# Fused chunk attention and swish MLP: a start-up wait moved behind a second load, and PV of one unit joined to the scores of the next from unit 14 on

## The chip, the cores and the metric

One core of a Trainium2 chip. The metric is the device time of one execution in microseconds (us). Lower is better. Each version was run several times on a chip beside runs of the kernel before; medians of all its runs are quoted with their number. A run is called fast or slow by its granted clock and by its distance from the fastest run of the same kernel.

## The reference, cut to what matters

```python
# q, k, v: (8, 8, 576, 64) float32; chunks of 64 positions attend within themselves
q_c = q.reshape(B, H, nc, chunk, D)          # the same for k_c, v_c; nc = 9
scores = scale * np.matmul(q_c, k_c.transpose(0, 1, 2, 4, 3))
attn = softmax(scores)                        # written out in the reference
out = np.matmul(attn, v_c).reshape(B, H, S, D)
x = out.transpose(0, 2, 1, 3).reshape(4608, 512)
h = x @ w_in                                  # (512, 2048)
g = h * (1.0 / (1.0 + np.exp(-beta * h)))
result = g @ w_out                            # (2048, 512), float32
```

## The kernel before

The 4608 tokens are worked in 18 units of 256, and the MLP in 9 blocks of two units. Everything is one static order. While TensorE works through the first layer of block j (`hps`) and the second layer of block j-1 (`ops`), pieces of the attention of later units are put in between: scores (`sc`), then PV (attention weights times v, into `x` or `y`). From unit 8 on both use the array as 64 x 64; the MLP uses it as 128 x 128. ScalarE makes the exponentials and the sigmoid, VectorE normalises and multiplies, and in the blocks shown below transposes go by DMA. GpSimd issues most loads. The results of the large matmuls go to a pool of four buffers (`ps_p`), called banks below.

The part that puts pieces in place, for blocks 3 to 8. The number at the head of each item is a place within the block, from 0 to 1:

```python
        def att_items(u, a0, w):
            return [(a0, 2, ("sc", u)), (a0 + 0.40 * w, 3, ("pv", u)),
                    (a0 + 0.41 * w, 3, ("norm", u, 0)), (a0 + 0.55 * w, 3, ("norm", u, 1)),
                    (a0 + 0.10 * w, 3, ("T", u + 1))]

        for j in range(3, NB):
            items = [(0.02 + 0.98 * m / KFF, 0, ("m", m)) for m in range(KFF)]
            # ... the second layer of block j-1, in eight parts ...
            if j + 1 < NB:
                for i in range(2):
                    items += att_items(2 * j + 2 + i, 0.03 + 0.43 * i, 0.43)
            items.sort(key=lambda it: it[:2])
            # ... each item is emitted in this order ...
```

The start. `emit_idle` and `emit_tiny` are matmuls on zeros that keep TensorE busy ahead of the first scores; the one that reads `late` waits for GpSimd's memset. In the kernel before, idle matmuls of 512 columns start 0.43 us apart up to about 7.7 us and 0.216 apart from 8.78 us on. Where this text says that the clock doubled, it means this change of spacing at the start: the granted clock of the profile reads 1.00 through the same twelve microseconds. That the idle matmuls bring the doubling on is what they are put there for.

```python
        # ... SyncE loads the first halves of q, k; GpSimd the second halves; SyncE beta ...
        nc.gpsimd.memset(late, 0.0)
        for i in range(4):
            load_v(i)
        # ... GpSimd: weights and further loads ...
        emit_tiny(78)
        warm = idle_bank()
        emit_idle(3, 512, warm)
        nc.tensor.matmul(out=warm[:, 0:16], lhsT=idle[:, 0:128], rhs=late)
        emit_idle(10, 512, warm)
        emit_T_half(0)          # ScalarE casts, VectorE transposes the first halves
        emit_sc_half(0, 0)      # 32 small matmuls
        emit_ex_half(0, 0)
        warm = idle_bank()
        emit_idle(6, 512, warm)
        emit_T_half(1)          # VectorE transposes the second halves
        nc.vector.transpose(out=bt, in_=braw)
        emit_sc_half(0, 1)
```

The softmax here doesn't subtract the row's maximum and nothing guards it: scores larger than these inputs give would overflow.

## Time and profile before

| | kernel before |
|---|---|
| median of 3 runs (lowest to highest) | 289.49 us (289.14 to 290.41) |
| span of the profiled run | 287.5 us |
| TensorE busy | 281.2 us, 98% |
| VectorE, ScalarE busy | 141.4 and 146.7 us, 49% and 51% |
| first large first-layer matmul starts | 15.62 us |
| last group of second-layer matmuls starts | 280.80 us |

How to read it: from 17 us to the end TensorE hardly ever stands still, so its stream is the bound. The start of the first large matmul says what the start-up cost. The start of the last group says where the stream ended, for the tail behind it is the same in every version (6.6 to 6.7 us to the end of the span in the seven that are read at this point: before, after, e2, e3, e4, e8 and e12). These are the two rows, in order of time (start, duration to the modelled end, engine, line, operation, tiles, shape, count, and in brackets the idle time before it with what ended it):

```profile
15.62 1.03 PE L322 MATMUL hps<-xt,win 128*128 128x256 f16 x8 [0.67 <-ACT xt L297]
280.80 3.70 PE L580 MATMUL ops<-wout,gt 128*128 128x256 f16 x48
```

Their distance is 265.18 us.

### The profile page before, as it was taken

How to read it: one execution, taken by the hardware profiler on the slowest of the kernel's cores; microseconds unless marked ns; L12 is line 12 of the kernel's file. 1: busy time of each engine (PE TensorE's matmuls, PEld its weight loads, DVE VectorE, ACT ScalarE, POOL GpSimd, SP SyncE). 2: the span in 40 equal slices, each digit the busy share in tenths (PEclk: the TensorE clock that was granted, in tenths of full speed). 3: DMA queues.
4: the chain of work that ended last, by engine and by line, in shares of the span. 5: the costliest groups of instructions: out<-in, count | busy, mean ns of one | idle time of the engine just before them, and what ended most of it. 6: DMA issues, size and time to landing. Idle time of an engine off the chain costs nothing.

```text
span 287.5 us, 6650 instructions
## 1 busy us (share of the span) xinstructions
PE 281.2 (98%) x2779; PEld 136.2 (47%) x2779; DVE 141.4 (49%) x253; ACT 146.7 (51%) x224; POOL 95.7 (33%) x125
## 2 busy tenths in 40 slices
PE   8889999999999999999999999999999999999995
PEld 4464456545544444444444444444444444444444
DVE  2678444776567554534454445444453536333300
ACT  4377218774557545454545454555445544444411
POOL 8743579397172992060907060000000000000000
PEclk9999999999999999999999999999999999999999
DMA  8999999999999999999999999614252212010012
GB/s 197 174 197 206 169 178 209 211 163 173 153 94 182 155 176 179 153 130 159 132 167 134 145 155 142 134 49 110 75 113 73 73 39 73 36 39 36 36 73 75
DMA packets 139997, 37.14 MB, mean 129 GB/s; under 512 B 126912, under 2 KB 135488, under 8 KB 139968
## 3 DMA queue, kind: packets, MB, share of 16 engines
q0 software_dynamic: 99136, 17.83, 79.7%
q1 hardware_dynamic: 40688, 18.83, 30.5%
q8 instruction: 22, 0.36, 0.5%
q14 instruction: 7, 0.06, 0.1%
q10 hardware_dynamic: 144, 0.07, 0.1%
HBM read 36.71 MB, written 9.44 MB: 161 GB/s over the span
## 4 chain that ended last, share of the span: by engine, by line
PE 94%; DMA 3%; ACT 1%; issue 1%; DVE 0%; POOL 0%; DVEq 0%; POOLq 0%
PE hps L322 44%; PE ops L354 42%; DMA h<-in_k_dram 3%; PE x L264 2%; PE sc L236 1%; PE sc L223 1%; PE ops L580 1%; ACT xt L297 1%; PE xp L296 1%; PE sc L196 0%; ACT et L206 0%; POOL h L394 0%; PE warm L374 0%; PE xp L304 0%; DVE xt L297 0%
## 5 line engine op out<-in xcount | busy, mean ns | idle before, releaser
L336 DVE SCALAR_TENSOR_TENSOR gt<-sg,hps 128x512 f16<-128x512 f32 (+1 forms) x153 | 99.1, 654 | 108.5 <-ACT sg L332 108.3
L332 ACT ACTIVATE sg<-hps,beta 128x512 f32<-128x512 f32 (+1 forms) x153 | 100.4, 663 | 74.0 <-PE hps L322 73.9
L322 PE MATMUL hps<-xt,win 128*128 128x512 f16 (+1 forms) x612 | 136.7, 367 | 0.8 <-ACT xt L297 0.7
L354 PE MATMUL ops<-wout,gt 128*128 128x512 f16 x560 | 131.3, 379 | 0.0
L322 PEld LDWEIGHTS <-win 128*128 128x128 f16 x612 | 58.0, 98 | 61.9 <-issue 1.0
L354 PEld LDWEIGHTS <-gt 128*128 128x128 f16 x560 | 53.7, 98 | 63.1
L364 ACT ACTIVATE osb<-ops 128x512 f32<-128x512 f32 x35 | 20.9, 598 | 42.2 <-PE ops L354 42.2
L112 POOL DMA_DIRECT2D vbig<-in_v_dram x40 | 34.0, 872 | 10.3 <-DMA wout<-in_moe_w_out_dram 3.7
L98 POOL DMA_DIRECT2D qu<-in_q_dram x22 | 18.7, 865 | 39.5 <-DMA qT<-qu 37.2
L280 DVE TENSOR_TENSOR x<-x,rd 128x512 f16<-128x512 f32 x34 | 23.5, 692 | 1.3
L98 POOL DMA_DIRECT2D ku<-in_k_dram x22 | 18.9, 880 | 0.1
L278 DVE RECIPROCAL rd<-x 128x8 f32<-128x8 f32 x34 | 6.8, 201 | 11.1 <-PE x L264 11.1
L245 ACT ACTIVATE et<-sc 128x1024 f16<-128x1024 f32 (+1 forms) x8 | 6.4, 811 | 8.2 <-PE sc L236 8.2
L229 ACT ACTIVATE et<-sc 128x1024 f16<-128x1024 f32 x10 | 10.1, 1015 | 0.0
L264 PEld LDWEIGHTS <-et 64*64 64x64 f16 x576 | 6.0, 107 | 7.3 <-issue 3.4
L374 PE MATMUL warm<-idle 128*128 128x512 f16 x24 | 8.6, 515 | 0.0
L264 PE MATMUL x<-vbig,et 64*64 64x65 f16 x544 | 7.8, 195 | 0.2 <-ACT et L206 0.2
L104 POOL DMA_DIRECT2D ku<-in_k_dram x9 | 6.8, 755 | 2.5 <-DMA win<-in_moe_w_in_dram 1.3
L104 POOL DMA_DIRECT2D qu<-in_q_dram x9 | 6.8, 767 | 1.9 <-DMA win<-in_moe_w_in_dram 1.1
L592 DVE TENSOR_SCALAR osb<-ops 128x256 f32<-128x256 f32 (+1 forms) x2 | 0.7, 358 | 12.1 <-PE ops L580 12.1
L130 POOL DMA_DIRECT2D win<-in_moe_w_in_dram x8 | 6.0, 751 | 1.2 <-DMA h<-in_k_dram 0.8
L177 DVE STREAM_TRANSPOSE t<-h 128x512 f32<-128x512 f32 x4 | 4.2, 1084 | 4.2 <-ACT h L176 3.7
(46 smaller groups left out, 69.3 us busy)
## 6 DMA issues: line engine op xcount, KB each, us to landing
out_dram<-osb SPq DMA_DIRECT2D x35, 256.0 KB, 3.4
vbig<-in_v_dram POOLq DMA_DIRECT2D x32, 128.0 KB, 7.6
qu<-in_q_dram POOLq DMA_DIRECT2D x20, 128.0 KB, 5.3
ku<-in_k_dram POOLq DMA_DIRECT2D x20, 128.0 KB, 6.6
win<-in_moe_w_in_dram POOLq DMA_DIRECT2D x8, 256.0 KB, 9.7
wout<-in_moe_w_out_dram POOLq DMA_DIRECT2D x4, 512.0 KB, 12.4
qu<-in_q_dram POOLq DMA_DIRECT2D x3, 256.0 KB, 7.3
ku<-in_k_dram POOLq DMA_DIRECT2D x3, 256.0 KB, 8.9
```

The costliest lines, as they stand in the source:

```text
L98: nc.gpsimd.dma_start(out=tv[off:off + n, sp], in_=src[b, :, s:s + n, :].rearrange("h p d -> p h d"),)
L104: nc.gpsimd.dma_start(out=t[off // 2:(off + n) // 2], in_=src[b, :, s:s + n, :].rearrange("h (p r) d -> p h r d", r=2),)
L112: nc.gpsimd.dma_start(out=vbig[off:off + n, i, :, 0:D], in_=v[b, :, s:s + n, :].rearrange("h p d -> p h d"),)
L229: nc.scalar.activation(out=et, in_=sc, func=ACTF.Exp, scale=scale)
L264: nc.tensor.matmul(out=(x[0][64 * c:64 * c + 64, r, g, 0:D + 1] if len(x) == 1 else x[r][64 * c:64 * c + 64, g, 0:D + 1]), lhsT=(et[64 * r ...
L280: nc.vector.tensor_tensor(out=o, in0=z[..., 0:D], in1=rd[:, r].to_broadcast(list(o.shape)), op=ALU.mult)
L322: nc.tensor.matmul(out=hps[:, 0:n], lhsT=w_in16[m // 2][:, kk, (m % 2) * 128:(m % 2) * 128 + 128], rhs=xr[:, c0 // CH:(c0 + n) // CH, 2 * ...
L332: nc.scalar.activation(out=sg[:, 0:n], in_=hps[:, 0:n], func=ACTF.Tanh, scale=beta2[:, m:m + 1])
L336: nc.vector.scalar_tensor_tensor(out=gt_t[j][:, m, c0:c0 + n], in0=sg[:, 0:n], scalar=1.0, in1=hps[:, 0:n], op0=ALU.add, op1=ALU.mult,)
L354: nc.tensor.matmul(out=ops, lhsT=gt_t[j][:, kk, t * 128:(t + 1) * 128], rhs=w_out16[kk // 4][:, kk % 4, :], start=(kk == 0), stop=(kk == K ...
L364: nc.scalar.activation(out=osb, in_=ops, func=ACTF.Copy, scale=0.5)
L374: nc.tensor.matmul(out=d[:, 0:w], lhsT=idle[:, 0:128], rhs=idle[:, 0:w])
```

## The change

Its intent: (1) to hold part of the start-up idle work back, so that TensorE's idle matmuls reach up to the first scores, and (2) to let PV of a unit and scores of the next share one passage between the 128 x 128 and the 64 x 64 use of the array, from unit 14 on. The diff, its core:

```diff
+    MU = 14
...
     def emit_pv(u, where=("x", "s")):
         et = et_t.pop(u)
-        for s in range(2):
+        for s in (1, 0) if u >= MU else (0, 1):
...
+    def emit_norms(u):
+        for s in (1, 0) if u >= MU else (0, 1):
+            emit_norm(u, s)
+            emit_xt_dma(u, s)
...
-        nc.gpsimd.memset(late, 0.0)
         for i in range(4):
             load_v(i)
+            if i == 1:
+                nc.gpsimd.memset(late, 0.0)
...
-            if j + 1 < NB:
+            if 2 * j + 2 < MU:
                 for i in range(2):
                     items += att_items(2 * j + 2 + i, 0.03 + 0.43 * i, 0.43)
+                if 2 * j + 4 == MU:
+                    items += [(0.89, 2, ("sc", MU)), (0.90, 3, ("T", MU + 1))]
+            elif j + 1 < NB:
+                for i in range(2):
+                    items.append((0.15 + 0.5 * i, 2, ("hop", 2 * j + 2 + i)))
...
+                elif it[0] == "hop":
+                    emit_pv(it[1], ("x", "p" if it[1] + 1 < NU else "s"))
+                    if it[1] + 1 < NU:
+                        emit_sc(it[1] + 1)
+                    if it[1] + 2 < NU:
+                        emit_T(it[1] + 2)
+                    emit_norms(it[1])
```

## The prediction

> **What bounds the kernel now.** I read the page's busy shares and its chain first, then one window of nearly the whole run, then the order of time of TensorE around the attention pieces, and last the first ten microseconds. The page:
>
> ```profile
> PE 281.2 (98%) x2779; PEld 136.2 (47%) x2779; DVE 141.4 (49%) x253; ACT 146.7 (51%) x224; POOL 95.7 (33%) x125
> PE 94%; DMA 3%; ACT 1%; issue 1%; DVE 0%; POOL 0%; DVEq 0%; POOLq 0%
> 17.00:285.00 268.00, 267.32 (x2463) 128.61 (x2461) 132.42 (x232) 139.38 (x214) 82.35 (x102) 1.00 1.10 126
> ```
>
> The second line is the chain that ended last: 94% of it is TensorE and 3% is one load of k at the start. The third is a row of the view by windows (start and end, length, then busy time of TensorE, weight loads, VectorE, ScalarE, GpSimd). From 17 to 285 us, TensorE is busy for 267.32 of 268.00 us, and the modelled end of its last matmul at about 284.5 us accounts for most of the missing 0.7. So there is no gap to fill after 17 us. Only a shorter TensorE stream can bring the end forward, and it does so one for one, because the tail after the last matmul is three small evictions and stores that the change leaves alone. VectorE and ScalarE at about half are not the bound.
>
> A TensorE busy 98% need not do useful work all that time. The order of time around units 16 and 17 (start, duration to the modelled end of the last, engine, line, operation, count):
>
> ```profile
> 200.69 1.89 PE L322 MATMUL hps<-xt,win 128*128 128x512 f16 x8
> 202.42 1.89 PE L354 MATMUL ops<-wout,gt 128*128 128x512 f16 x8
> 204.24 0.45 PE L264 MATMUL x<-vbig,et 64*64 64x65 f16 x32
> 204.62 1.90 PE L322 MATMUL hps<-xt,win 128*128 128x512 f16 x8
> ...
> 214.99 1.03 PE L322 MATMUL hps<-xt,win 128*128 128x512 f16 x4
> 215.94 0.45 PE L223 MATMUL sc<-qT,kT 64*64 64x64 f16 x32
> 216.32 1.04 PE L322 MATMUL hps<-xt,win 128*128 128x512 f16 x4
> ...
> 219.88 0.31 PE L264 MATMUL x<-vbig,et 64*64 64x65 f16 x14
> 219.88 0.41 PE L264 MATMUL x<-vbig,et 64*64 64x65 f16 x27
> ```
>
> Eight large matmuls take 202.42 - 200.69 = 1.73 us, 0.216 each. Eight large ones with a PV piece behind them take 204.62 - 202.42 = 2.20, so one piece of 32 small matmuls costs 0.47 us. Scores cost the same: 216.32 - 214.99 = 1.33, less 4 x 0.216 = 0.86, is 0.47. The last two rows are the same piece cut off at 220.00 and at 220.10: 13 more had started in 0.10 us, 7.7 ns each, so 32 of them start within about 0.26 us. The other 0.2 us of each piece is passage: about 0.09 us at its start (204.24 against 202.42 + 1.73 = 204.15) and about 0.12 between its last start (near 220.14) and the next large matmul at 220.26. This 0.2 us is what the second part of the change is after.
>
> [...] the pieces use the array as 64x64, their neighbours as 128x128, and each border shows about 0.1 us. [...] idle matmuls of 512 columns are 0.43 us apart before 7.7 us and 0.216 apart after 8.7 us. The row of granted clock says 1.00 all the time, so this halving is not in that row. [...] loads and the memset follow each other without overlap of more than 0.04 us.
>
> **The change, part by part.** *Second part.* For units 14 to 17 the kernel before has eight pieces: scores and PV of each, all apart. The built order of the changed kernel has five: scores 14 alone, PV 14 with scores 15, PV 15 with scores 16, PV 16 with scores 17, PV 17 alone. TensorE has the same number of instructions. Three pairs of pieces become one each, so three passages in and three out go: at most 3 x 0.2 = 0.6 us. If only the entry (0.09) is saved [...], 3 x 0.1 = 0.3. There is one further cost. In a merged piece PV of the second half goes to two banks of the pool of four that the large matmuls use. The built order then gives the next accumulation of the second layer the bank of the last first-layer block before the piece, where before it had an older one. That block must be through ScalarE and VectorE first (after the PV piece at 219.88):
>
> ```profile
> 219.99 0.69 ACT L332 ACTIVATE sg<-hps,beta 128x512 f32<-128x512 f32 x1 [0.27 <-PE hps L322]
> 220.70 0.69 DVE L336 SCALAR_TENSOR_TENSOR gt<-sg,hps 128x512 f16<-128x512 f32 x1 [1.75 <-ACT sg L332]
> ```
>
> It is free at 220.70 + 0.69 = 221.39 plus a few hundredths for the semaphore. A merged piece starting at 219.88 would take 0.26 + 0.26 + 0.12 = 0.64, the next block of four 0.86, so the accumulation wants the bank at 221.38. I put 0.05 us of new wait on each, 0.15 in all. On VectorE three normalisations are split in two (0.17 + 0.42 twice, in place of 0.20 + 0.69, so 0.3 us more each), and they now stand ahead of the next product; VectorE has over 1 us idle there, and the banks are wanted later than they come free (the two PV banks by about 222.6, their next users start at 223.2 and 224.1). Sum of this part: between -0.6 and -0.15, taken as -0.45 us.
>
> *First part.* The start, by all engines:
>
> ```profile
> 2.86 0.15 POOL L401 MEMSET late<- 128x16 f16 x1
> 2.90 3.54 POOL L112 DMA_DIRECT2D vbig<-in_v_dram  x4
> 3.37 0.22 PE L417 MATMUL warm<-late,idle 128*128 128x16 f16 x1
> 3.44 4.41 PE L374 MATMUL warm<-idle 128*128 128x512 f16 x10
> 8.40 0.45 PE L196 MATMUL sc<-t,t 32*64 32x64 f16 x32 [0.55 <-DVE t L177]
> 8.78 1.47 PE L374 MATMUL warm<-idle 128*128 128x512 f16 x6
> 9.77 1.08 DVE L177 STREAM_TRANSPOSE t<-h 128x512 f32<-128x512 f32 x1 [0.50 <-DMA h<-in_k_dram]
> 10.91 0.71 PE L196 MATMUL sc<-t,t 32*64 32x64 f16 x64 [0.66 <-DVE bt L425]
> ```
>
> Now the matmul at 3.37 waits for nothing: the memset ended at 3.01. Behind two v loads of 3.54 / 4 = 0.885 us the memset runs at about 2.88 + 1.77 = 4.65 to 4.80, so the ten idle matmuls begin near 4.9 instead of 3.44, and TensorE stands still for 1.4 us. That in itself is off the path: the first scores wait for VectorE until 8.40, and the next ones, at 10.91, hang on the k load that landed at 9.75. What decides is the clock. If it doubles at the same moment (between 7.7 and 8.4 here), about 7 idle ones are done by 8.0, and three more at 0.216 end at 8.65; scores and six idle ones end at 8.65 + 0.38 + 1.30 = 10.3, before 10.91, and nothing is lost. If all ten run slow they end at 4.9 + 4.3 = 9.2 and the path is touched. The loads of v go out 0.04 us earlier, which is nothing. I take 0 for this part, with an expected loss of about 0.1 from the uncertain clock.
>
> Sum: 289.49 - 0.45 + 0.1, about 289.1 us.
>
> **The rivals.** *The pause delays the clock.* [...] Worst case, an estimate from the durations above: scores at 9.2 take twice 0.38, then six idle ones at 0.43 end at 12.5 where 10.91 was wanted, 1.6 us lost, giving about 290.7. *The pause helps.* The runs before span 289.14 to 290.41, and the gap from 7.7 to 8.4 may be what spoils some of them; idle work that now reaches up to the scores would close it. Then the slow draws vanish, and the median could fall by another 0.3 to 0.6, to 288.6. *A bank wait takes the place of the passages.* If PV has to wait for its two banks, or the next accumulation for its own by 0.2 us, the second part is worth nothing: 289.5. Against: by the built order the two PV banks belong to products over 1 us old. *Scores next to PV still pay a border.* Then 0.1 a pair is all, 289.3.
>
> **Range and chances.** The second part has a narrow range, -0.6 to 0. The clock adds -0.6 to +1.6, the low part of that unlikely, and medians of three runs of this kernel move by some tenths. So I predict 289.1 us, with 288.3 to 290.2 to hold it 8 times in 10. Two per cent would be 5.8 us; nothing here is near it: 0.01 faster, 0.98 within, 0.01 slower.
>
> **What would show each step right or wrong.** In the order of time of TensorE, the merged pieces should hold 32 PV and 32 scores whose starts follow without a gap, and from the large matmul before to the large one after should take 0.47 x 2 - 0.2 = 0.74 us over the plain stream; 0.84 means that a border stayed, 0.94 no gain. A wait for VectorE ahead of a second-layer accumulation after a merged piece would show the bank rival. The matmul on the late tile should move from 3.37 to about 4.9, and its ten followers show when the clock doubled: if the scores of the first half stay at about 8.4 to 8.7 and those at 10.91 stay, the first part is free; if either slips by more than a few tenths, the pause cost time. I would be wrong as a whole if the end moved by over 1 us with the start at 17 us unmoved, which I have no step for.

That PV and scores side by side have no border between them was the assumption, and the 0.2 us per saved passage in the 0.45 (3 x 0.2, less 0.15 for the banks) rests on it; the kernel before has no such pair to read it from. That a pause delays the doubling is a bare rival, with the worst case of 1.6 us that is worked out from the durations read; that a gap in TensorE's idle work spoils some runs ("the pause helps") was a guess. The few hundredths for a semaphore can be read from the kernel before: VectorE's transpose `bt` ends at 10.71 + 0.17 = 10.88 us, and the scores that wait for it start at 10.91.

## More of the kernel before

One row more of this kernel will be needed, from the list of DMA issues (size, and us from issue to landing), for GpSimd's load of the second half of k:

```profile
h<-in_k_dram POOLq DMA_DIRECT2D x1, 256.0 KB, 7.6
```

## The result, and the profile after

| | before | after |
|---|---|---|
| median of 6 runs each, same rounds | 289.40 us | 288.78 us |
| lowest to highest | 289.11 to 290.41 | 288.23 to 289.31 |
| span of the profiled run | 287.5 us | 286.7 us |
| first large first-layer matmul | 15.62 us | 15.33 us |
| last group of second-layer matmuls | 280.80 us | 280.04 us |

The ratio of fast runs, after to before, is 0.9975 (95% interval 0.9954 to 0.9995), within 2%. A ratio here is always the mean time of one kernel's fast runs over the mean of the other's in the same rounds, so it is not quite the ratio of the medians in the table.

The page of the changed kernel (busy shares and the chain that ended last), and then its row of the view by windows from 17 to 285 us:

```profile
PE 280.5 (98%) x2779; PEld 136.4 (48%) x2779; DVE 141.8 (49%) x259; ACT 146.9 (51%) x224; POOL 95.7 (33%) x125
PE 96%; ACT 1%; POOL 1%; issue 1%; DVE 0%; DVEq 0%; POOLq 0%
```

```profile
17.00:285.00 268.00, 266.56 (x2461) 128.60 (x2458) 132.76 (x237) 139.23 (x214) 82.34 (x102) 1.00 1.13 126
```

TensorE has the same 2779 matmuls, and it is still the bound. The 3% of the chain that was a DMA is gone: the chain no longer passes through the load of k. The two points of the stream:

```profile
15.33 1.03 PE L328 MATMUL hps<-xt,win 128*128 128x256 f16 x8 [0.67 <-ACT xt L303]
280.04 3.70 PE L599 MATMUL ops<-wout,gt 128*128 128x256 f16 x48
```

The end came 0.76 us earlier. Of that 0.29 was there at the first large matmul, and 0.47 came between the two points (264.71 us against 265.18).

**Where the 0.47 comes from.** The order of time of TensorE around the second merged piece:

```profile
203.69 1.03 PE L328 MATMUL hps<-xt,win 128*128 128x512 f16 x4
204.65 0.32 PE L265 MATMUL y<-vbig,et 64*64 64x65 f16 x16
204.80 0.30 PE L265 MATMUL x<-vbig,et 64*64 64x65 f16 x16
204.93 0.48 PE L224 MATMUL sc<-qT,kT 64*64 64x64 f16 x32
205.35 1.04 PE L328 MATMUL hps<-xt,win 128*128 128x512 f16 x4
```

PV and scores follow each other: 0.28 us lie between the start of PV (204.65) and that of the scores (204.93), near the 0.26 in which 32 starts fit. From the large matmul before to the large one after are 205.35 - 203.69 = 1.66 us; less four large matmuls, 0.863, that is 0.80 for the piece. The first and third merged pieces take 0.79 and 0.81. Two separate pieces took 2 x 0.47 = 0.94. So each pair saves 0.13 to 0.15, and three save 0.43.

The bank that the prediction watched, behind the third merged piece (all engines, the rows of the product, of its sigmoid and of the accumulation that takes its bank):

```profile
219.37 0.69 ACT L338 ACTIVATE sg<-hps,beta 128x512 f32<-128x512 f32 x1 [0.27 <-PE hps L328]
...
219.98 1.04 PE L328 MATMUL hps<-xt,win 128*128 128x512 f16 x4
220.09 0.69 DVE L342 SCALAR_TENSOR_TENSOR gt<-sg,hps 128x512 f16<-128x512 f32 x1 [1.90 <-ACT sg L338]
...
220.85 1.03 PE L360 MATMUL ops<-wout,gt 128*128 128x512 f16 x4
```

The product ends at 220.09 + 0.69 = 220.78. TensorE is through its four large matmuls at 219.98 + 0.86 = 220.84, and the accumulation starts at 220.85. There is no wait, with 0.06 us to spare.

**Where the 0.29 comes from.** The start of the changed kernel, rows of TensorE, GpSimd and VectorE:

```profile
2.12 1.46 PE L380 MATMUL warm<-idle 128*128 128x512 f16 x3
4.82 0.17 PE L424 MATMUL warm<-late,idle 128*128 128x16 f16 x1 [1.24 <-POOL late L410]
4.84 4.07 PE L380 MATMUL warm<-idle 128*128 128x512 f16 x10
7.27 2.94 DVE L178 STREAM_TRANSPOSE t<-h 128x512 f32<-128x512 f32 x3 [0.41 <-ACT h L177]
8.84 0.45 PE L197 MATMUL sc<-t,t 32*64 32x64 f16 x32
9.22 1.47 PE L380 MATMUL warm<-idle 128*128 128x512 f16 x6
10.62 0.71 PE L197 MATMUL sc<-t,t 32*64 32x64 f16 x64
```

The pause is there, 1.24 us, and the first scores slip from 8.40 to 8.84. But the second scores start at 10.62, not 10.91, and they no longer wait for anything. VectorE's third transpose, that of the second half of k, stood in the kernel before at 9.77 after 0.50 us of waiting for the load; now it follows the two others without a wait. The load has become faster:

```profile
h<-in_k_dram POOLq DMA_DIRECT2D x1, 256.0 KB, 6.6
```

6.6 us where the kernel before had 7.6, for the same load at the same place of the queue. No step of the prediction had this, and most of the experiments on the start ask why.

### The profile page after: what moved, and what is told of

The parts are those of the page before. It is cut to its first block, busy times and chain, and to the rows that moved or that the text cites. A ratio compares the mean times of both kernels' runs of the same rounds, so it can differ in the third digit from the quotient of the medians.

```text
span 286.7 us, 6657 instructions
## 1 busy us (share of the span) xinstructions
PE 280.5 (98%) x2779; PEld 136.4 (48%) x2779; DVE 141.8 (49%) x259; ACT 146.9 (51%) x224; POOL 95.7 (33%) x125
## 4 chain that ended last, share of the span: by engine, by line
PE 96%; ACT 1%; POOL 1%; issue 1%; DVE 0%; DVEq 0%; POOLq 0%
PE hps L328 44%; PE ops L360 43%; PE warm L380 2%; PE x L265 2%; PE sc L237 1%; PE sc L224 1%; PE ops L599 1%; ACT xt L303 1%; PE xp L302 1%; POOL h L400 1%; POOL vbig L113 1%; PE sc L197 0%; ACT et L207 0%; PE y L265 0%; PE xp L310 0%
## 5 line engine op out<-in xcount | busy, mean ns | idle before, releaser
L113 POOL DMA_DIRECT2D vbig<-in_v_dram x40 | 34.0, 870 | 10.9 <-DMA wout<-in_moe_w_out_dram 3.7
L286 DVE TENSOR_TENSOR x<-x,rd 128x512 f16<-128x512 f32 x31 | 21.4, 692 | 1.2
L284 DVE RECIPROCAL rd<-x 128x8 f32<-128x8 f32 x31 | 6.2, 201 | 12.5 <-PE x L265 12.5
L303 ACT COPY xt<-xp 128x512 f16<-128x512 f16 x9 | 5.1, 588 | 2.3 <-PE xp L302 2.2
```

Of the source, the lines that this page charges most:

```text
L113: nc.gpsimd.dma_start(out=vbig[off:off + n, i, :, 0:D], in_=v[b, :, s:s + n, :].rearrange("h p d -> p h d"),)
L286: nc.vector.tensor_tensor(out=o, in0=z[..., 0:D], in1=rd[:, r].to_broadcast(list(o.shape)), op=ALU.mult)
```

## The experiments

Twelve kernels ran, on four chips, each with a profile and each correct against the reference. All were timed beside the kernel before on their own chip. Its medians were 289.26 (11 runs; first chip), 289.23 (11; second), 289.14 (11; third) and 289.23 us (9; fourth, one of which was a slow run of 417.48 us at a granted clock of 0.659 that no ratio uses).

### The two parts apart: e1 and e2

e1_memset is the kernel before with the memset moved, and nothing else:

```diff
-        nc.gpsimd.memset(late, 0.0)
         for i in range(4):
             load_v(i)
+            if i == 1:
+                nc.gpsimd.memset(late, 0.0)
```

> Only the memset moved behind the second v load; the attention pieces as before. Theory A (the gain of the profiled pair was 0.45 us from three saved passages, and 0.29 us at the start is chance of when the k load landed): no difference, within 0.2 us of before. Theory B (the pause of TensorE or the order on GpSimd makes the start 0.3 us shorter): 0.3 us faster, with the first large matmul of the first layer at about 15.3 us in place of 15.6. Theory C (the pause delays the doubling of the clock in some runs): slower, in some runs by over 0.5 us.

Measured: median 289.42 us of 6 runs (288.72 to 290.05), ratio 1.0005 (0.9991 to 1.0018). The k load landed in 6.8 us. Yet the first large matmul started at 15.85, later than before, and the order of time of TensorE says why:

```profile
4.85 4.43 PE L374 MATMUL warm<-idle 128*128 128x512 f16 x10
9.21 0.60 PE L196 MATMUL sc<-t,t 32*64 32x64 f16 x32
9.74 1.47 PE L374 MATMUL warm<-idle 128*128 128x512 f16 x6
11.14 0.71 PE L196 MATMUL sc<-t,t 32*64 32x64 f16 x64
```

All ten idle matmuls ran at 0.43 us each and the scores behind them were slow too (0.60 where 0.45 is usual): in this run the clock doubled only after 9.3 us. In the profiled run of the changed kernel it had doubled by about 8.4 (its last three idle matmuls ahead of the scores start at 7.78, 8.21 and 8.53). What follows: this part brings an earlier k load and risks a later doubling, and over six runs the two cancel.

e2_hops is the kernel before with all of the diff but the memset:

```diff
     # the changed kernel, with the memset in its old place
+        nc.gpsimd.memset(late, 0.0)
         for i in range(4):
             load_v(i)
-            if i == 1:
-                nc.gpsimd.memset(late, 0.0)
```

> Only PV and scores merged from unit 14 on; the memset where it was. Theory A: the whole gain, 0.4 to 0.5 us faster than before, and about the time of the changed kernel. Theory B: 0.3 us slower than the changed kernel. In the trace each of three merged pieces should again take 0.79 to 0.81 us over the plain stream of large matmuls.

Measured: median 288.83 us of 5 runs (288.65 to 289.04), ratio 0.9987 (0.9975 to 0.9999). The three merged pieces took 0.79 to 0.80 us again. The first large matmul started at 15.75 and the last group at 280.44, 264.69 us apart (the changed kernel: 264.71). So the whole gain behind the start belongs to the merged pieces: 0.43 us in the medians, 0.49 between the points.

### Is it the passage? e3 and e4

The rival: something else in the new placing (other times for the transposes, the norms, the banks) brings the gain. e3_border keeps all of it, but puts one block of four large matmuls between PV and scores:

```diff
                     items.append((0.15 + 0.5 * i, 2, ("hop", 2 * j + 2 + i)))
+                    items.append((0.21 + 0.5 * i, 2, ("hopsc", 2 * j + 2 + i)))
...
                 elif it[0] == "hop":
                     emit_pv(it[1], ("x", "p" if it[1] + 1 < NU else "s"))
+                    emit_norms(it[1])
+                elif it[0] == "hopsc":
                     if it[1] + 1 < NU:
                         emit_sc(it[1] + 1)
                     if it[1] + 2 < NU:
                         emit_T(it[1] + 2)
-                    emit_norms(it[1])
```

> The changed kernel, but with one first-layer block of four large matmuls between PV and scores of each merged piece, so that both borders are back while the PSUM banks, the order of halves and the normalisation are as in the changed kernel. If the saved passages are the gain: 0.45 us slower than the changed kernel (0.15 for each of three), equal to the kernel with only the memset moved. If the gain came from anything else in the second part (banks, order of halves): no slower than the changed kernel.

Measured: median 289.29 us of 6 runs (289.01 to 290.05), ratio 1.0007 (0.9995 to 1.0019). Between the two points lie 280.60 - 15.42 = 265.18 us, exactly the kernel before's. The order of time of TensorE around the first of the pairs shows both borders back:

```profile
190.13 0.32 PE L265 MATMUL y<-vbig,et 64*64 64x65 f16 x16
190.28 0.30 PE L265 MATMUL x<-vbig,et 64*64 64x65 f16 x16
190.51 1.04 PE L328 MATMUL hps<-xt,win 128*128 128x512 f16 x4
191.47 0.45 PE L224 MATMUL sc<-qT,kT 64*64 64x64 f16 x32
191.85 1.47 PE L360 MATMUL ops<-wout,gt 128*128 128x512 f16 x6
```

PV takes 190.51 - 190.13 = 0.38 and the scores 191.85 - 191.47 = 0.38 to the next large matmul, and the scores start 0.10 after the four large ones are through (190.51 + 0.863 = 191.37).

e4_split goes the other way. It is the kernel before with PV of units 8 to 17 in two halves of 16 matmuls, with large matmuls between: ten more pieces, the same matmuls.

```diff
-            return [(a0, 2, ("sc", u)), (a0 + 0.40 * w, 3, ("pv", u)),
+            return [(a0, 2, ("sc", u)), (a0 + 0.40 * w, 3, ("pv", u, 0)), (a0 + 0.545 * w, 3, ("pv", u, 1)),
...
-    def emit_pv(u, where=("x", "s")):
-        et = et_t.pop(u)
-        for s in range(2):
+    def emit_pv(u, where=("x", "s"), halves=(0, 1)):
+        et = et_t[u]
+        for s in halves:
```

> The kernel before, with PV of units 8 to 17 cut into its two halves of 16 matmuls with large matmuls between them: ten more pieces, the same instructions otherwise. If a passage of a piece costs 0.15 us: 1.5 us slower than before. If it costs 0.2 us: 2.0 us slower. If TensorE hides the borders and the gain is elsewhere: no difference.

Measured: median 291.43 us of 4 runs (291.39 to 291.59), ratio 1.0078 (1.0065 to 1.0091): 2.17 us over the kernel before in the medians, 0.22 for each further piece. Between its two points lie 282.98 - 15.50 = 267.48 us, 2.30 more. One half piece in its order of time:

```profile
190.63 1.03 PE L322 MATMUL hps<-xt,win 128*128 128x512 f16 x4
191.59 0.32 PE L264 MATMUL x<-vbig,et 64*64 64x65 f16 x16
191.84 1.04 PE L322 MATMUL hps<-xt,win 128*128 128x512 f16 x4
```

191.84 - 190.63 - 0.863 = 0.35 us for 16 small matmuls. By the 7.7 ns per start of the prediction these need 0.12; the rest, 0.22, is passage. So a passage costs 0.22 us when one is added and 0.13 to 0.15 came back for each that was taken away. That the passage is the cause is shown from both sides.

### Why the k load lands earlier: e6, e9, e10, e11

Three theories. *Pause*: TensorE standing still frees something. *Order*: the memset stood between GpSimd's loads of k and v, and without it the queue runs better. *Fetch*: the profile has a DMA queue that it calls `q8 instruction`, with 22 transfers of 0.36 MB in all, 16 KB each; if they bring TensorE's instructions, one of them falls into the k load or behind it, depending on when TensorE gets past its wait for `late`. For the third there is a row in the view of the DMA queues, in windows of half a microsecond (queue, packets, MB, share of 16 engines). First the kernel before from 7.0 to 7.5 us, then the changed kernel from 8.5 to 9.0:

```profile
q8 instruction: 1, 0.02, 11.7%
```

```profile
q8 instruction: 1, 0.02, 12.2%
```

One packet of 0.02 MB in each: 0.117 x 16 x 0.5 = 0.94 and 0.98 us of one engine's time. The bursts in the view put its start at 7.16 us before and at 8.68 after. Before, that lies within the flight of the k load, which landed near 9.75; after, it begins as the load lands, whose last part is recorded at 8.69. (The bursts give a start to about 0.02 us.) That the queue is TensorE's own is inferred from e10 and e11 below: against e2, which has its transfer between 7.0 and 7.5 us, they change nothing but the number of TensorE's tiny and idle matmuls, and the transfer moves to 12.59 us with 31 fewer and to 5.56 with 31 more. With the 31 fewer the queue also has 21 transfers where e2 has 22.

e6_nowait is the changed kernel without the pause: the matmul reads the idle tile, the memset stays behind the second v load.

```diff
-        nc.tensor.matmul(out=warm[:, 0:16], lhsT=idle[:, 0:128], rhs=late)
+        nc.tensor.matmul(out=warm[:, 0:16], lhsT=idle[:, 0:128], rhs=idle[:, 0:16])
```

> The changed kernel (memset behind the second v load, merged pieces), but the late matmul reads the idle tile, so it waits for nothing: no pause of TensorE. In the six traces so far the second k load landed 7.5 to 7.8 us after its issue where the memset stands directly behind it, and 6.6 to 6.8 where the memset stands behind the v loads. Theory order (the place of the memset on GpSimd lets the load land sooner): 6.7 us here too, the second scores at about 10.5 us in every run, 0.3 to 0.4 us faster than the kernel with only the merged pieces, about 288.5. Theory pause (the still TensorE lets the load land sooner): 7.6 us here, and the time of the kernel with only the merged pieces, about 288.8. In both, runs should lie within 0.5 us of each other, as TensorE is busy from 2.1 us on.

Measured: median 288.86 us of 6 runs (288.52 to 289.33), ratio 0.9977 (0.9948 to 1.0006). The instruction transfer came at 5.40 us and the k load took 7.4. The memset is moved here just as in the changed kernel and the load is slow again, so moving the memset doesn't by itself make the load fast.

e9_two_memsets is the changed kernel with one more memset, of another tile, in the old place directly behind the k load:

```diff
+    late0 = const.tile([128, 16], FP16)
...
+        nc.gpsimd.memset(late0, 0.0)
         for i in range(4):
             load_v(i)
```

> The changed kernel with a second memset of another tile put back directly behind the k load; the late matmul waits for the later one. Theory order: the k load lands after 7.6 us again although TensorE pauses, the second scores start at 10.9 us or later, and the median is 289.0 to 289.5, with a spread of about 1 us from the clock. Theory pause: the load lands after 6.7 us and the time is that of the changed kernel.

Measured: median 289.57 us of 6 runs (288.44 to 290.48), ratio 0.9996 (0.9965 to 1.0027); transfer at 8.69 us, k load 6.6 us. GpSimd's order around the loads is that of the kernel before again, and the load is fast. With e6 this refutes the theory of order. The clock doubled late in the profiled run, as in e1: ten idle matmuls in 4.43 us, second scores at 11.22.

e10_tiny46 is e2 (memset in its old place, no pause) with 46 tiny matmuls and four idle ones where there were 78 and three, so that TensorE is further back in its instructions at every moment of the start:

```diff
-        emit_tiny(78)
+        emit_tiny(46)
         warm = idle_bank()
-        emit_idle(3, 512, warm)
+        emit_idle(4, 512, warm)
```

> Merged pieces, memset directly behind the k load as before, no pause; 46 in place of 78 tiny matmuls at the start and four in place of three idle ones, so that TensorE is as busy but has 62 instructions fewer up to the late matmul. In ten traces the one 16 KB transfer of TensorE's instruction queue takes 0.9 to 1.0 us; where it starts at 8.9 us or later the second k load lands 6.6 to 6.8 us after its issue, where it starts at 5.6 to 7.6 us the load lands after 7.4 to 7.8. Theory fetch: fewer instructions ahead move that transfer later; if it moves past 8.8 us, the load lands after 6.7 us without any pause, and the kernel takes about 288.5. Theory pause (the still TensorE itself): 7.4 to 7.8 us wherever the transfer lies, and 288.8.

Measured: the k load landed in 6.6 us, with no pause at all, and the transfer came at 12.59 us. This refutes the pause as such. (The expectation has the transfers of the earlier traces some 0.2 us later than they are read here; the order is the same.) The time, though, went the wrong way: median 293.28 us of 6 runs (292.04 to 294.45), ratio 1.0138 (1.0110 to 1.0167). The order of time of TensorE, and then the row of windows from 15 to 17 us (the number behind the five engines is the granted clock):

```profile
11.86 0.41 PE L197 MATMUL sc<-t,t 32*64 32x64 f16 x26
14.93 0.31 PE L197 MATMUL sc<-t,t 32*64 32x64 f16 x6 [2.66 <-issue]
```

```profile
15.00:17.00 2.00, 2.00 (x17) 0.91 (x16) 0.00 (x0) 1.02 (x1) 1.48 (x3) 0.50 1.45 196
```

TensorE stops in the middle of a run of equal matmuls for 2.66 us, waiting for nothing that the profile shows, and goes on 2.34 us after the late transfer started. Up to the stop the trace has 223 matmuls and as many weight loads. The stop begins at 14.93 - 2.66 = 12.27 us, just before the transfer starts at 12.59. That TensorE ran out of instructions and waited for this transfer is the author's reading, and it fits this order; the profile doesn't say it. Behind the stop the clock is granted at 0.50.

e11_tiny110 goes the other way, with 110 tiny and two idle ones:

```diff
-        emit_tiny(78)
+        emit_tiny(110)
         warm = idle_bank()
-        emit_idle(3, 512, warm)
+        emit_idle(2, 512, warm)
```

> The reverse: 110 tiny matmuls and two idle ones, 62 instructions more up to the late matmul. Theory fetch: the transfer comes at 5.6 us or earlier; if it lies wholly before the last packets of the k load it still delays one engine's share, so 7.4 us or so; if it falls before 3 us the load lands after 6.7 us. Theory pause: 7.4 to 7.8 us. The time within 0.3 us of the kernel with only the merged pieces.

Measured: median 288.69 us of 6 runs (288.60 to 289.75), ratio 0.9985 (0.9969 to 1.0000). Transfer at 5.56 us, well within the flight of the k load, which took 7.6 us.

Over all fourteen traces the rule has no exception:

| instruction transfer starts (us) | kernels | k load, issue to landing (us) |
|---|---|---|
| 5.40 to 7.36 | before, e2, e4, e6, e7, e8, e11 | 7.4 to 7.8 |
| 8.68 to 12.59 | after, e1, e3, e5, e9, e10, e12 | 6.5 to 6.8 |

The step between the rows, about 0.9 us, is about the length of the transfer (0.94 and 0.98 us above). This is a correlation with the right size, with the two rivals refuted.

One thing more speaks for it. The packed trace keeps 16 landing times for each load, as many as there are DMA engines. In the kernels of the first row one or two of the 16 parts of the k load land late, at 9.26 to 9.88 us, and all the others by 8.91; in those of the second row all 16 land by 8.96. In e6 and e11, where the transfer came early, one part of the q load before it is late as well (8.26 and 8.42, the others by 7.27). So the load as a whole is not slower: a part or two of 16 are held up, by 0.5 to 1.3 us, as would be so if one engine were occupied.

In five of the seven kernels of the second row the transfer starts within 0.3 us of the landing, so it might seem to wait for the load; but it comes 3.8 to 4.1 us after TensorE is past its wait for `late`, as it does in the kernel before (7.16 against 3.37). That the late part and the transfer sat on the same DMA engine stays argued: the trace doesn't keep the packets by engine.

### Pause and clock: e5 and e12

e5_memset4 is the changed kernel with the memset behind the fourth v load:

```diff
-            if i == 1:
+            if i == 3:
                 nc.gpsimd.memset(late, 0.0)
```

> The changed kernel with the memset behind the fourth v load: TensorE stands still until about 6.4 us in place of 4.8. If a pause delays the doubling of the clock and the idle matmuls then hold up the scores: the ten idle ones end at 8.5 to 10.7, first scores at 9 to 10.8, second ones at 11 to 12.8, so 0.5 to 1.5 us slower than the changed kernel, with a spread of over 1 us. If the pause is harmless: no slower than the changed kernel.

Measured: median 290.70 us of 6 runs (289.85 to 291.30), ratio 1.0033 (1.0004 to 1.0063).

```profile
6.58 0.17 PE L424 MATMUL warm<-late,idle 128*128 128x16 f16 x1 [3.00 <-POOL late L410]
6.61 4.43 PE L380 MATMUL warm<-idle 128*128 128x512 f16 x10
```

The pause is 3.00 us, the ten idle matmuls all run slow and end near 10.9, and the second scores start at 13.31. The k load landed in 6.7 us, and it was worth nothing. Against the changed kernel this start cost 2.7 us in the profiled runs and 1.9 in the medians. So in these runs a pause was harmless only where the idle work behind it ended before the operands were there.

e12_late6 tries to keep the early k load without the pause. Six idle matmuls stand ahead of the one that waits and seven behind it, so that the memset is done when TensorE comes to it:

```diff
-        emit_idle(3, 512, warm)
+        emit_idle(6, 512, warm)
         nc.tensor.matmul(out=warm[:, 0:16], lhsT=idle[:, 0:128], rhs=late)
-        emit_idle(10, 512, warm)
+        emit_idle(7, 512, warm)
```

> The changed kernel with the waiting matmul three idle matmuls later (six ahead of it, seven behind, in place of three and ten): TensorE reaches it at about 4.7 us, when the memset behind the second v load is just done, so the wait is there but the pause is not (0.1 us in place of 1.24). If the instruction transfer follows the end of that wait by 4.1 to 4.5 us, as in the traces so far, it starts at about 9 us, the k load lands 6.7 us after its issue, [...] and the second scores start at about 10.3 us: 0.6 us less at the start and 0.45 from the merged pieces, 288.2 to 288.4, with a spread of about 0.5 us. If TensorE must stand still for the early landing, or the transfer goes back to 7.4 us: 288.8.

Measured: median 288.83 us of 5 runs (288.45 to 289.01), ratio 0.9981 (0.9967 to 0.9995): no better than the changed kernel or e2. The start did what it should. The k load landed in 6.5 us, the second scores started at 10.20 and the first large matmul at 15.02, 0.60 us before the kernel before's. But the last group stood at 280.50, behind the changed kernel's. The order of time of TensorE shows where most of it went:

```profile
126.51 1.02 PE L328 MATMUL hps<-xt,win 128*128 128x512 f16 x4 [0.43 <-DMA xt<-x]
```

At the head of this block TensorE waits for the DMA transpose of the block's input; the changed kernel has no such wait there. In all 0.58 us are lost at this place, and a further 0.2 in a slow piece of scores at 43.43 us. It is not that TensorE outran a transfer that came as usual: the transfer was issued 0.25 us earlier than in the changed kernel (121.07 against 121.32) and took 5.2 us to land where it took 2.5 there, and 3.8 in the kernel before. Why it was slow is open. This is one profiled run, the slowest of the five, and whether the others lost as much at the same place isn't shown.

### Can more pieces be merged? e8 and e7

e8_mu10 and e7_mu12 are e2 with the merging from unit 10 and from unit 12 on.

```diff
-    MU = 14
+    MU = 10
```

> The kernel with only the merged pieces, with merging from unit 10 on: seven merged pieces in place of three. At the measured 0.15 us each: 0.6 us faster than with three, about 288.2. Rival: the scores of units 11 to 17 now come about a third of a block (9 us) earlier, while the loads still fill the DMA queues; then TensorE waits for a transpose of q or k, and it is no faster or slower by the length of the wait.

Measured: median 293.73 us of 6 runs (292.88 to 294.67), ratio 1.0140 (1.0109 to 1.0171). The order of time of TensorE, and then the row of windows from 134.6 to 138 us:

```profile
134.62 0.45 PE L224 MATMUL sc<-qT,kT 64*64 64x64 f16 x32 [3.09 <-DMA qT<-qu]
```

```profile
134.60:138.00 3.40, 3.38 (x40) 1.44 (x41) 0.38 (x1) 1.71 (x2) 2.98 (x4) 0.57 1.78 172
```

Scores that stand next to PV of the unit before are wanted sooner, and here their transposed q isn't there: 3.09 us of wait. (The loads do fill the DMA engines then, as the expectation has it: in the kernel before their mean busy share is 80% or more in each slice of the page up to 179 us.) Behind it the clock is granted at 0.57 over 3.4 us, which is 0.43 x 3.4 = 1.5 us of lost work. Against e2 the last group is 4.02 us late (284.46 against 280.44). Wait and clock make 4.6, less four more pairs at 0.15, which is 4.0. That is not all: the first large matmul of this run came 0.26 us earlier than e2's (15.49 against 15.75), so its stream lost 4.28, and the clock is still at 0.76 from 138 to 139 us, 0.24 us more; 0.1 is left over.

```diff
-    MU = 14
+    MU = 12
```

> The kernel with only the merged pieces, with merging from unit 12 on: five merged pieces. In the trace of merging from unit 10 the one stall was at the first piece, where q of unit 11 had not landed (3.1 us); the later pieces had none. If unit 12 is late enough: two more passages saved, 0.3 us faster than with three merged pieces, 288.5. If q of unit 13 is not there yet: slower by the wait.

Measured: median 293.61 us of 6 runs, and in two groups: 289.72 in the profiled run, 293.41 to 294.18 in the five others (granted clock 0.999 in the first and 0.993 or 0.994 in the five; two of the five count as slow by their distance of over 1.5%). The ratio of fast runs is 1.0113 (1.0067 to 1.0158). The profiled run has the same wait, short:

```profile
162.37 0.45 PE L224 MATMUL sc<-qT,kT 64*64 64x64 f16 x32 [0.68 <-DMA qT<-qu]
```

The others have no trace. Their 4 us and their lower clock look like the longer wait of e8, which is a guess. What is shown is that merging from unit 12 on or earlier makes TensorE wait for operands, and that from unit 14 on it doesn't.

## Why the prediction was right or wrong

The predicted time was 289.1 us and the measured median is 288.78, inside the range; the sum of the second part holds, and the first part has the right net and an incomplete mechanism.

| step of the prediction | what it put | what the runs showed |
|---|---|---|
| only a shorter TensorE stream moves the end | one for one | held: last group 0.76 earlier, span 0.8 shorter |
| merged piece over the plain stream | 0.74, or 0.84 if a border stays | 0.79, 0.80, 0.81 |
| new wait for a bank, each | 0.05 | none; bank free 0.06 us before it is wanted |
| second part in sum | -0.45 (-0.6 to -0.15) | -0.47 between the points; -0.43 in e2's medians |
| pause of TensorE, first scores | 1.4 us; 8.65 | 1.24 us; 8.84 |
| second scores stay at 10.91, hung on the k load | no change | 10.62; the k load landed 1.0 earlier |
| first part in sum | 0, expected loss 0.1 | -0.29 in the profiled run; e1 1.0005 over six runs |

**Second part.** The mechanism was right, and e3 and e4 show it as the cause. Two terms of the sum were off and cancel, so that the sum is this close is partly luck. The saving of a merged piece was put between 0.1 and 0.2, with 0.2 taken for the aim; it measured 0.13 to 0.15, for the starts inside a merged piece do not keep the pace of separate ones: PV takes 0.28 to 0.34 us to the scores where its 32 starts need 0.26, and the scores 0.41 to 0.42 to the next large matmul, in two of three, where a separate piece takes 0.38. What stretches them is open. The wait of 0.05 us for a bank did not occur: the prediction let the merged piece take 0.64 from its start to the next large matmul; it takes 0.69 to 0.72, and the product came as early as foreseen (1.52 us behind the piece's start in the third).

The rival "a bank wait takes the place of the passages" is refuted by the trace, and "scores next to PV still pay a border" at its full size by the 0.28 in which PV is followed by scores in two of three. But the pieces measured 0.79 to 0.81, midway between the 0.74 of no border and the 0.84 of a whole one, and in the third 0.34 - 0.26 = 0.08 us lie between PV and scores, nearly the 0.09 of an entry. So about half a border is still paid, and what it consists of isn't shown.

**First part.** The step that failed is "the next ones, at 10.91, hang on the k load that landed at 9.75", taken as fixed. Everything else moved around it as foreseen, but the landing itself changes with what TensorE does, by way of its instruction transfer as far as the traces tell. With the load 1.0 us earlier the second scores hang on TensorE's own idle matmuls: 9.22 + 6 x 0.216 + 0.1 = 10.6. The clock rival was right in kind, though no run shows why the doubling came late: in the profiled runs of e1 and e9 all ten idle matmuls ran slow (4.43 us, where the changed kernel's took 4.07) and the path was touched, by 0.2 to 0.3 us at 10.91, not by the worst case of 1.6, since the six idle ones behind the scores ran fast in both (1.47 us for six). So the expected zero is right as the sum of two effects, of which the prediction had one; that it came out is luck. The 0.29 of the profiled pair also stands beside 0.26 by which single traces of one and the same start differ: in the five kernels with the old one (before, e2, e4, e7, e8) the first large matmul comes at 15.49 to 15.75. The rival "the pause helps", put at 0.3 to 0.6 us, isn't seen: e1's interval ends at 0.9991, which is 0.26 us.

Whether the start adds to the merged pieces over many runs is open. The changed kernel, with it, has 0.9975, and e2, without it, 0.9987, with intervals that overlap. Runs with a pause look more spread (ranges of 1.08, 1.33, 1.04, 1.45 and 2.04 us for after, e1, e3, e5 and e9; 0.39, 0.20, 0.81, 1.15 and 0.56 for e2, e4, e6, e11 and e12), which would fit two competing effects, an earlier k load and a doubling that came by 8.4 us in one profiled run (after) and only after 9.3 in another (e1), but the kernel before itself ranged over 0.55 us on the first chip and 2.54 on the second.

One line of the start was misread, without effect on the sum: the memset (2.86 to 3.01) overlaps the first v load (from 2.90) by 0.11 us, not by 0.04 at most. They still start in order (2.86, then 2.90), which is all that this step needs.

## What to carry to other kernels

When TensorE is the bound, look for small pieces that use the array in another mode, and put those of one mode side by side: each passage saved is worth what the trace shows for it (here 0.13 to 0.15 us of 0.2), and a wait of 3 us for operands that aren't there yet costs twenty times as much, with the clock on top (in e8 3.09 us of wait, and behind it a granted clock of 0.57 over 3.4 us). An idle or waiting TensorE at the start is not free of effects on others: here, with a pause of 1.24 us, an instruction transfer that is taken to be its own came at 8.68 us instead of 7.16, and with it went, as far as the traces tell, the landing of a load (6.6 us after its issue instead of 7.6). Before a move at the start is credited or blamed, measure it alone, for two effects of a few tenths can cancel.
